# Output sums of an FFT filter and Swish layer: tokens stationary, or output weights stationary and turned by DMA

## The chip, the cores and the metric

The kernel runs on one core of a Trainium2 chip. The metric is the device time of one execution in microseconds. Three runs of the kernel before gave 775.34 to 776.41 us, with a median of 775.49 us. A core has five engines that run side by side, each with its own instruction queue taken in order: TensorE (PE; its weight loads are shown as PEld), VectorE (DVE), ScalarE (ACT), GpSimd (POOL) and SyncE (SP), which here only issues DMAs.

## The reference, cut to what matters

```python
def _attn_ref(x, filt_r, filt_i):            # x: 8 x 3008 x 256
    X = np.fft.rfft(x, axis=1)
    Y = X * (filt_r + 1j * filt_i)[None, :, :]
    return np.fft.irfft(Y, n=x.shape[1], axis=1)

def _moe_ref(x, w_in, w_out, beta):          # x: 24064 x 256, d_ff = 2048
    h = x @ w_in
    g = h / (1.0 + np.exp(-beta * h))
    return g @ w_out                         # 24064 x 256, float32
```

A long convolution along the sequence of each batch (the mixing) is followed by a two-layer network on every token.

## The kernel before, in words

**The network, which sets the pace.** The 24064 tokens are 47 blocks of 512 (`TB`). A block has 16 steps, one for each group of 128 hidden features (`NFB`), so there are 752 steps in all (`NSTEP`), and the main loop runs over them in order. Step `s` of block `i` forms the hidden values of one group: two matmuls of 512 columns into `hps` (line L784; four shorter ones where a block holds tokens of two batches), then ScalarE's activation into `gT` (L793). Two steps later (`lags`) the output sums take this `gT` (L802): four matmuls, one for each 128 tokens, with `gT` as the stationary operand and 256 columns of `wout_sb` streamed, into one of two accumulators of the block, `acc[i, 0]` and `acc[i, 1]`. Each is one bank, and the pool `opsum` has three. After the last group of a block, at step 16k + 1, `out_block` copies both accumulators to `ost` on VectorE (L112) and SP stores them to the output (L761 or L763).

**The mixing, woven in.** The transform of one batch is cut into short products that are planned into the steps of the batch before it. `at(step, fn, ...)` puts a call into the list of a step; the main loop runs a step's list after its hidden matmuls and before its output sums. Let `o` be the first step of the batch before (a multiple of 16); steps of a batch are counted from it. The stages are:

- `load_x` (L171): POOL issues the loads of x.
- `s1` (L564): products on x, evacuated to `a1` (one buffer). `a2_load` (L580): SP issues eight transposing DMAs from `a1` to `a2`, two for each quarter.
- `s2` (L591, L605 to L610): products, then three VectorE operations that apply the filter, then an addition on POOL that makes `yh`.
- `s3` (L623): products on `yh`, evacuated to `z`; after each six rows of the spectrum SP stores `z` to a scratch tensor `d` in DRAM (L630, written d<-z).
- `zz_load` (L635): SP loads `d` back in another order, in four quarters, each when the stores have landed. `s4` (L645): products on `zz`, evacuated to `y`, from which the next hidden values come.

For batches 3 to 7, `s2` stands at steps 4, 8 and 12 of each 16 up to step 60, `s3` six steps later (so the last is at 66), `zz_load` at 70, `s4` at 80 to 92, `a2_load` at 82. Batch 2 differs only in its first six `s2`. Batch 1, in the first 80 steps, has `s2` about two steps apart from step 23 to 46, `s3` five steps after it, `zz_load` at 54 and `s4` from 66. Batch 0 is mixed before the main loop.

**What sets the order.** Each engine takes its instructions in the order in which the code emits them. So SP's queue mixes output stores, d<-z stores, zz loads and transposing DMAs, and POOL's mixes the `yh` additions with the issues of x loads. An instruction that waits holds up all behind it on its queue, though not on other engines. The pool `wst` (three buffers of 4 KB a partition, tag `ws`) serves the loads of the output weights at the start, and nothing later.

The last block (steps 736 to 751) has its own ending in `out_last`.

Of the kernel before, what the change touches and what calls it, by code (L numbers as in the profile page):

```python
# [10 lines left out]
P = 128  # L11
# [4 lines left out]
F32 = mybir.dt.float32  # L16
BF16 = mybir.dt.bfloat16
I32 = mybir.dt.int32

TWO_PI = 2.0 * math.pi  # L20

# [15 lines left out]
def kernel(  # L37
# [10 lines left out]
    nc = tc.nc  # L48

    B, S, D = x.shape  # L50
# [50 lines left out]
    wout_sb = wpool.tile([P, NFB, D], BF16, name="wout_sb", tag="wout_sb")  # L101
# [4 lines left out]
    st = {}  # L106

    def evac(dst, src, on_act, scale=None):
        if on_act:
            nc.scalar.activation(dst, src, ACT.Copy, scale=1.0 if scale is None else scale)  # L110
        elif scale is None:
            nc.vector.tensor_copy(dst, src)  # L112
        else:
            nc.vector.tensor_scalar_mul(dst, src, scale)  # L114
# [23 lines left out]
    def small(name, dt=F32):  # L138
        return sp.tile([P, 1], dt, name=name, tag=name)
# [8 lines left out]

    ip = sp.tile([P, 1], I32, name="ip", tag="ip")
    warm = small("warm")  # L150
# [44 lines left out]
    def shift_and(name, sh, mask, eng=None):  # L195
        t = small(name, I32)
        eng = eng or nc.vector
# [150 lines left out]
    wst = ctx.enter_context(tc.tile_pool(name="wstage", bufs=3, **tw))  # L348
# [337 lines left out]
    for b in range(1, B):  # L686
        o = first_step[b - 1]
        if b == 1:
            at(1, z_late, 1, 0)
            at(2, z_late, 1, 1)  # L690
            s1_steps(1, range(16), [4 + (2 * i + 1) // 3 for i in range(16)], False, (1, 4, 7, 10, 13))
            for i, r in enumerate((3, 4, 5, 6)):
                at(r, f_late, 1, i // 2, i % 2)
            for g in range(NG):
                at(o + 16, a2_load, 1, g)
            for hh, z0, f0 in ((2, (6, 9), (12, 15, 16, 17)), (3, (17, 18), (19, 20, 21, 22))):
                for e in range(NDC):
                    at(z0[e], z_late, hh, e)
                for i, r in enumerate(f0):
                    at(r, f_late, hh, i // 2, i % 2)  # L700
            s23_steps(1, [o + r for r in (23, 25, 27, 29, 31, 34, 36, 38, 40, 42, 44, 46)], 5, 1)
            for h in range(J // JG):
                at(o + 54, zz_load, 1, h)
            s4_steps(1, [o + 66 + (i * 12) // 15 for i in range(16)], 2)
            at(0, scale_wout, 2 * WG)
            at(0, load_wout, 3 * WG)
            at(1, scale_wout, 3 * WG)
            if B > 2:
                for g in range(4):
                    at(o + 24 + 3 * g, load_x, 2, g)  # L710
                late = (54, 55, 56, 57, 58, 59, 60, 61, 66, 67, 68, 70, 72, 73, 74, 76)
                s1_steps(2, range(16), [o + r for r in late], False)
                for g in range(NG):
                    at(o + 80, a2_load, 2, g)
                if B > 3:
                    for g in range(4):
                        at(o + (62, 68, 88, 92)[g], load_x, 3, g)
            continue
        base = [o + 16 * n + s for n in range(4) for s in (4, 8, 12)]
        if b == 2:  # L720
            base[:6] = [o + r for r in (8, 12, 19, 22, 26, 29)]
        s23_steps(b, base, 6, False)
        for h in range(J // JG):
            at(o + 70, zz_load, b, h)
        s4_steps(b, [o + 80 + (i * 13) // 15 for i in range(16)], False)
        if b + 1 < B:
            early = [o + 16 * n + s for n in range(4) for s in (7, 13)]
            late = [o + s for s in (66, 67, 69, 70, 72, 73, 75, 76)]
            s1_steps(b + 1, range(16), early + late, False)
            for g in range(NG):  # L730
                at(o + 82, a2_load, b + 1, g)
            if b + 2 < B:
                for g in range(4):
# [12 lines left out]
    def acc_of(i, tb):  # L746
        h = tb if i == NBLK - 1 and tb == 3 else tb // 2
        if (i, h) not in acc:
            acc[i, h] = opsum.tile([P, 2, D], F32, name="acc", tag="acc")
        return acc[i, h]  # L750

    def out_block(i):
        ost = ostp.tile([P, 4, D], F32, name="ost", tag="ost")
        rows = out[i * TB : (i + 1) * TB, :].rearrange("(c p) d -> p c d", p=P)
# [8 lines left out]
        nc.sync.dma_start(rows, ost[:])  # L763

    def out_last(i, tb, ost):
        rows = out[i * TB : (i + 1) * TB, :].rearrange("(c p) d -> p c d", p=P)
        if tb == 1:
            evac(ost[:, :2, :], acc[i, 0][:], True)
            nc.sync.dma_start(rows[:, :2, :], ost[:, :2, :])
        elif tb > 1:  # L770
            evac(ost[:, tb, :], acc_of(i, tb)[:, tb % 2, :], False)
            (nc.scalar if tb == 2 else nc.sync).dma_start(rows[:, tb, :], ost[:, tb, :])

    for s in range(NSTEP + 4):
        if s < NSTEP:
            i, fb = divmod(s, NFB)
            t0 = i * TB
            hps = hpsum.tile([P, TB], F32, name="hps", tag="hps")
            pos = t0
            while pos < t0 + TB:  # L780
                b, n0 = divmod(pos, S)
                ln = min(S - n0, t0 + TB - pos)
                for dc in range(NDC):
                    nc.tensor.matmul(  # L784
                        hps[:, pos - t0 : pos - t0 + ln],
                        lhsT=win_sb[:, dc, fb * P : (fb + 1) * P],
                        rhs=ys[b][:, dc, n0 : n0 + ln],
                        start=(dc == 0),
                        stop=(dc == NDC - 1),
                    )  # L790
# [9 lines left out]
        for i, fb, tb in outs.get(s, ()):  # L800
            lone = i == last and tb > 1
            nc.tensor.matmul(  # L802
                acc_of(i, tb)[:, tb % 2, :],
                lhsT=blk[i * NFB + fb][:, tb * P : (tb + 1) * P],
                rhs=wout_sb[:, fb, :],
                start=(fb == 0 and (tb % 2 == 0 or lone)),
                stop=(fb == NFB - 1),
                skip_group_check=True,
            )
            if fb == NFB - 1:  # L810
                if i == last:
                    out_last(i, tb, ost)
                elif tb == 3:
                    out_block(i)
# [1 line left out]
_INS = ['x', 'filt_r', 'filt_i', 'moe_w_in', 'moe_w_out', 'moe_beta']  # L816
_OUTS = [((24064, 256), 'float32')]
# [25 lines left out]
```

## Time and profile before

| what | value |
|---|---|
| median of three runs | 775.49 us |
| the profiled execution's own time | 775.0 us |
| its span on the core | 773.0 us |
| granted TensorE clock | 0.999 |
| busy: PE, PEld, DVE, ACT, POOL | 757.8, 549.6, 433.3, 552.3, 151.1 us |
| DMA: moved, mean rate | 77.74 MB, 101 GB/s |
| transposing DMAs of `a2_load` | 56, median 1.287 us to issue, 2.8 us to landing |

The span is the time between the first and the last instruction of the profiled execution, and the execution's own time is some 2 us longer. Times in a timeline count from the start of the span. A line names the source line, the engine, the operation, the tiles written and read, and their shape. SPq and POOLq are DMA issues on the queues of SP and POOL; their duration is that of the issue, not of the transfer. "Landing" is the time from the issue to the end of the transfer. Matmuls are pipelined, so that the durations of two neighbours overlap; the distance between starts is what counts.

### The profile page before, as it was taken

The numbers are of one execution on the slowest core, as the hardware profiler recorded it, in microseconds if no ns is written. First come the engines' busy times: TensorE is split into PE (matmuls) and PEld (weight loads), VectorE is DVE, ScalarE is ACT, GpSimd is POOL, SyncE is SP. The second block draws the span as 40 slices with busy tenths as digits, with TensorE's granted clock in tenths as the row PEclk, the third lists the DMA queues.
The fourth block names the chain that finished last, engine by engine and source line by source line (L and its number), as shares of the span: only waits on it lengthen the run. The fifth ranks groups of instructions, "written<-read, shape, count | busy, mean of one in ns | idle before, by whom it ended". The sixth has DMA issues, their size and how long they took to land.

```text
span 773.0 us, 15801 instructions
## 1 busy us (share of the span) xinstructions
PE 757.8 (98%) x6286; PEld 549.6 (71%) x6383; DVE 433.3 (56%) x716; ACT 552.3 (71%) x813; POOL 151.1 (20%) x154
## 2 busy tenths in 40 slices
PE   8899999999999999999999999999999999999997
PEld 5677777677776777877778777776777766676665
DVE  8879654765556655667456664566745665321001
ACT  7767877776677766776767776677766777777776
POOL 6804301312012210122101322022200222000000
PEclk9999999999999999999999999999999999999999
DMA  9959475234813258141681317621146111500101
GB/s 199 245 111 154 124 171 114 69 113 88 192 51 88 76 122 176 32 116 50 149 152 64 82 48 178 130 68 48 49 130 137 49 49 48 157 29 28 56 28 55
DMA packets 104125, 77.74 MB, mean 101 GB/s; under 512 B 49692, under 2 KB 97052, under 8 KB 104052
## 3 DMA queue, kind: packets, MB, share of 16 engines
q1 hardware_dynamic: 97652, 63.19, 31.6%
q0 software_dynamic: 4192, 13.40, 10.2%
q8 instruction: 50, 0.82, 0.4%
q10 hardware_dynamic: 2208, 0.14, 0.2%
q14 instruction: 23, 0.19, 0.1%
HBM read 43.46 MB, written 35.65 MB: 102 GB/s over the span
## 4 chain that ended last, share of the span: by engine, by line
PE 96%; ACT 1%; DVE 1%; issue 1%; POOL 0%; DVEq 0%; POOLq 0%
PE acc L802 44%; PE hps L784 39%; PE ps L645 3%; PE ps L564 3%; PE ps L591 3%; PE ps L623 3%; PE sps L444 0%; PE tp L393 0%; ACT aT L110 0%; ACT t L110 0%; ACT y L110 0%; PE ps L398 0%; DVE u L226 0%; DVE pq_t L430 0%; PE sps L423 0%
## 5 line engine op out<-in xcount | busy, mean ns | idle before, releaser
L793 ACT ACTIVATE gT<-hps,beta_sb 128x512 bf16<-128x512 f32 x752 | 516.8, 687 | 208.1 <-PE hps L784 184.3
L802 PE MATMUL acc<-wout_sb,gT 128*128 128x256 bf16 x3008 | 453.2, 272 | 2.3
L784 PE MATMUL hps<-y,win_sb 128*128 128x512 bf16 (+7 forms) x1633 | 427.4, 350 | 0.1
L802 PEld LDWEIGHTS <-gT 128*128 128x128 bf16 x3008 | 281.0, 98 | 101.9 <-issue 0.9
L610 POOL TENSOR_TENSOR yh<-a_t,b_t 128x512 bf16<-128x512 f32 x84 | 106.6, 1269 | 421.4 <-DVE b_t L609 421.0
L784 PEld LDWEIGHTS <-win_sb 128*128 128x128 bf16 x1728 | 164.7, 98 | 24.5 <-DVE y L114 0.3
L112 DVE COPY ost<-acc 128x512 f32<-128x512 f32 (+1 forms) x94 | 60.0, 680 | 139.8 <-PE acc L802 139.7
L114 DVE TENSOR_SCALAR y<-ps 128x376 bf16<-128x376 f32 (+2 forms) x128 | 63.3, 510 | 62.2 <-PE ps L645 59.1
L605 DVE TENSOR_TENSOR a_t<-ps,fr_sb 128x512 f32<-128x512 f32 x84 | 58.1, 692 | 67.7 <-PE ps L591 67.2
L112 DVE CAST a<-ps 128x384 bf16<-128x384 f32 x107 | 59.1, 557 | 57.2 <-PE ps L564 46.8
L606 DVE SCALAR_TENSOR_TENSOR b_t<-ps,fi_sb 64x512 f32<-64x512 f32 x84 | 58.2, 693 | 1.1
L609 DVE TENSOR_TENSOR b_t<-ps,fi_sb 64x512 f32<-64x512 f32 x84 | 57.4, 684 | 1.1
L112 DVE CAST z<-ps 128x512 bf16<-128x512 f32 x72 | 49.4, 686 | 1.9 <-PE ps L623 1.0
L645 PEld LDWEIGHTS <-zz 96*128 96x128 bf16 x448 | 29.7, 97 | 22.9
L564 PEld LDWEIGHTS <-xg 94*128 94x128 bf16 x448 | 30.4, 97 | 19.9 <-DMA xg<-in_x_dram 0.2
L564 PE MATMUL ps<-t,xg 94*128 94x96 bf16 x448 | 36.7, 205 | 0.7
L645 PE MATMUL ps<-t,zz 96*128 96x94 bf16 x448 | 34.7, 205 | 1.2
L623 PE MATMUL ps<-yh,t 128*128 128x256 bf16 x168 | 32.1, 273 | 0.4
L591 PE MATMUL ps<-a,t 128*128 128x256 bf16 x168 | 32.1, 273 | 0.4
L623 PEld LDWEIGHTS <-t 128*128 128x128 bf16 x168 | 16.2, 98 | 17.7 <-issue 0.6
L591 PEld LDWEIGHTS <-t 128*128 128x128 bf16 x168 | 16.1, 98 | 16.1
L171 POOL DMA_DIRECT2D xg<-in_x_dram x24 | 12.5, 523 | 54.9 <-PE ps L564 54.9
(95 smaller groups left out, 175.9 us busy)
## 6 DMA issues: line engine op xcount, KB each, us to landing
out_dram<-ost SPq DMA_DIRECT2D x42, 512.0 KB, 3.0
d<-z SPq DMA_DIRECT2D x28, 384.0 KB, 3.7
zz<-d SPq DMA_DIRECT2D x28, 384.0 KB, 6.8
xg<-in_x_dram POOLq DMA_DIRECT2D x24, 384.0 KB, 4.9
out_dram<-ost SPq DMA_DIRECT2D x9, 256.0 KB, 3.4
ws<-in_moe_w_out_dram SPq DMA_DIRECT2D x4, 512.0 KB, 7.8
fr_sb<-in_filt_r_dram SPq DMA_DIRECT2D x12, 128.0 KB, 4.3
fi_sb<-in_filt_i_dram SPq DMA_DIRECT2D x12, 128.0 KB, 4.3
```

The lines of the kernel that those rows point to most:

```text
L112: nc.vector.tensor_copy(dst, src)
L114: nc.vector.tensor_scalar_mul(dst, src, scale)
L564: nc.tensor.matmul(ps[:, m * KP : (m + 1) * KP], lhsT=xg[b, g][:NP, m0 + m, e * P : (e + 1) * P], rhs=t1[:], start=True, stop=True,)
L591: nc.tensor.matmul(ps[:, e, :], lhsT=t2[:, k0 + e, :], rhs=st["a2", b, g][:, kk + e, :], start=True, stop=True,)
L605: nc.vector.tensor_tensor(a_t[:], ps[:], fr_sb[:, ks, :], ALU.mult)
L606: nc.vector.scalar_tensor_tensor(b_t[:M], ps[M:], -1.0, fi_sb[M:, ks, :], ALU.mult, ALU.mult)
L610: nc.gpsimd.tensor_tensor(yh[:], a_t[:], b_t[:], ALU.add)
L623: nc.tensor.matmul(ps[:, e, :], lhsT=t3[:, 2 * i + e, :P], rhs=yh[:, e, :], start=True, stop=True)
L645: nc.tensor.matmul(ps[:, e, :NP], lhsT=zz[:, j0 % JG + e, dc * P : (dc + 1) * P], rhs=t4[:], start=True, stop=True,)
L784: nc.tensor.matmul(hps[:, pos - t0 : pos - t0 + ln], lhsT=win_sb[:, dc, fb * P : (fb + 1) * P], rhs=ys[b][:, dc, n0 : n0 + ln], start=(dc ...
L793: nc.scalar.activation(gT[:], hps[:], ACT.Silu, scale=beta_sb[:, fb : fb + 1])
L802: nc.tensor.matmul(acc_of(i, tb)[:, tb % 2, :], lhsT=blk[i * NFB + fb][:, tb * P : (tb + 1) * P], rhs=wout_sb[:, fb, :], start=(fb == 0 an ...
```

## The change

For all blocks but the last, the output sums swap their operands. The stationary operand is now a 128 x 128 piece of the output weights, and the 512 tokens of `gT` are streamed: two matmuls of 512 columns a step instead of four of 256. The sums then stand turned, with output features on the partitions and tokens along them, and have to be turned back before they are stored:

1. `out_turn(i)`, at step 16k + 1. For each of the two accumulators VectorE copies it to `of`; POOL splits its 32-bit values into two planes of 16-bit halves, `pl`; SP issues a transposing DMA of 128 x 1024 16-bit values from `pl` to `xb`.
2. `out_block(i)`, planned eleven steps later. POOL joins the two planes of `xb` to 32-bit values in `ost`, in two copies, and SP stores `ost` as before.

`of`, `pl` and `xb` take the three buffers of `wst` in turn. The four quarters of `a2_load` are no longer issued together: they stand four steps apart, from step 80 or 82 (17, 19, 24 and 30 for batch 1). The steps of `s1` for batch 1 move by one. The last block keeps the old form.

```diff
-            s1_steps(1, range(16), [4 + (2 * i + 1) // 3 for i in range(16)], False, (1, 4, 7, 10, 13))
+            s1_steps(1, range(16), [5 + (2 * i + 1) // 3 for i in range(16)], False, (1, 4, 7, 10, 13))
...
-                at(o + 16, a2_load, 1, g)
+                at(o + (17, 19, 24, 30)[g], a2_load, 1, g)
...
-                    at(o + 80, a2_load, 2, g)
+                    at(o + 80 + 4 * g, a2_load, 2, g)
...
-                at(o + 82, a2_load, b + 1, g)
+                at(o + 82 + 4 * g, a2_load, b + 1, g)
...
-    lags = {i: (2, 2, 2, 2) for i in range(NBLK)}
+    lags = {i: (2, 2) for i in range(NBLK)}
...
+    def out_turn(i):
+        of = wst.tile([P, NDC, TB], F32, name="ws", tag="ws")
+        pl = wst.tile([P, NDC, 2, TB], U16, name="ws", tag="ws")
+        xb = wst.tile([P, 2, 4, D], U16, name="ws", tag="ws")
+        for dc in range(NDC):
+            evac(of[:, dc, :], acc[i, dc][:].rearrange("p a d -> p (a d)"), False)
+            nc.gpsimd.tensor_copy(
+                pl[:, dc],
+                of[:, dc, :].bitcast(U16).rearrange("p (t q) -> p q t", q=2),
+            )
+            nc.sync.dma_start_transpose(
+                xb[:, :, :, dc * P : (dc + 1) * P].rearrange("p q c d -> p (q c) d"),
+                pl[:, dc].rearrange("p q t -> p (q t)"),
+            )
+        st["xb", i] = xb
+
     def out_block(i):
+        xb = st.pop(("xb", i))
         ost = ostp.tile([P, 4, D], F32, name="ost", tag="ost")
...
         for h in range(2):
-            evac(ost[:, 2 * h : 2 * h + 2, :], acc[i, h][:], False)
+            cs = slice(2 * h, 2 * h + 2)
+            nc.gpsimd.tensor_copy(
+                ost[:, cs, :].rearrange("p c d -> p (c d)").bitcast(U16).rearrange("p (c q) -> p c q", q=2),
+                xb[:, :, cs, :].rearrange("p q c d -> p (c d) q"),
+            )
...
+        for i, fb, q in outs.get(s, ()):
+            gT = blk[i * NFB + fb]
+            if i < last:
+                nc.tensor.matmul(
+                    acc_of(i, q)[:].rearrange("p a d -> p (a d)"),
+                    lhsT=wout_sb[:, fb, q * P : (q + 1) * P],
+                    rhs=gT[:],
+                    start=(fb == 0),
+                    stop=(fb == NFB - 1),
+                )
+                if fb == NFB - 1 and q == 1:
+                    out_turn(i)
+                    at(s + 11, out_block, i)
+                continue
```

More of the change, by code (lines that the diff above doesn't have):

```diff
@@ L18 @@
 I32 = mybir.dt.int32
+U16 = mybir.dt.uint16
 TWO_PI = 2.0 * math.pi
@@ L744, with acc_of @@
             outs.setdefault(min(s + lag, NSTEP + max(1, tb)), []).append((i, fb, tb))
-    def acc_of(i, tb):
-        h = tb if i == NBLK - 1 and tb == 3 else tb // 2
+    def acc_of(i, h):
         if (i, h) not in acc:
@@ L750, in acc_of, with last_acc @@
         return acc[i, h]
+    def last_acc(tb):
+        return acc_of(NBLK - 1, tb if tb == 3 else tb // 2)
+    def out_turn(i):
[13 more added lines that the diff above has]
+        st["xb", i] = xb
     def out_block(i):
+        xb = st.pop(("xb", i))
         ost = ostp.tile([P, 4, D], F32, name="ost", tag="ost")
-        rows = out[i * TB : (i + 1) * TB, :].rearrange("(c p) d -> p c d", p=P)
         for h in range(2):
-            evac(ost[:, 2 * h : 2 * h + 2, :], acc[i, h][:], False)
+            cs = slice(2 * h, 2 * h + 2)
[3 more added lines that the diff above has]
+            )
         if i < HB:
@@ L762, in out_block @@
             return
-        nc.sync.dma_start(rows, ost[:])
+        nc.sync.dma_start(out[i * TB : (i + 1) * TB, :].rearrange("(c p) d -> p c d", p=P), ost[:])
     def out_last(i, tb, ost):
@@ L770, in out_last @@
         elif tb > 1:
-            evac(ost[:, tb, :], acc_of(i, tb)[:, tb % 2, :], False)
+            evac(ost[:, tb, :], last_acc(tb)[:, tb % 2, :], False)
             (nc.scalar if tb == 2 else nc.sync).dma_start(rows[:, tb, :], ost[:, tb, :])
@@ L799 @@
             ost = ostp.tile([P, 4, D], F32, name="ost", tag="ost")
-        for i, fb, tb in outs.get(s, ()):
-            lone = i == last and tb > 1
+        for i, fb, q in outs.get(s, ()):
[12 more added lines that the diff above has]
+                continue
             nc.tensor.matmul(
-                acc_of(i, tb)[:, tb % 2, :],
-                lhsT=blk[i * NFB + fb][:, tb * P : (tb + 1) * P],
+                last_acc(q)[:, q % 2, :],
+                lhsT=gT[:, q * P : (q + 1) * P],
                 rhs=wout_sb[:, fb, :],
-                start=(fb == 0 and (tb % 2 == 0 or lone)),
+                start=(fb == 0 and (q % 2 == 0 or q > 1)),
                 stop=(fb == NFB - 1),
@@ L810 @@
             if fb == NFB - 1:
[L811 to L814, printed above, removed]
+                out_last(i, q, ost)
 _INS = ['x', 'filt_r', 'filt_i', 'moe_w_in', 'moe_w_out', 'moe_beta']
```

## The prediction

> **What bounds the kernel now.** I read the busy table first, then the chain that ended last, then the groups, and last the timeline around the places where work comes from a DMA. From the page:
>
> ```profile
> span 773.0 us, 15801 instructions
> ...
> PE 757.8 (98%) x6286; PEld 549.6 (71%) x6383; DVE 433.3 (56%) x716; ACT 552.3 (71%) x813; POOL 151.1 (20%) x154
> ...
> PE 96%; ACT 1%; DVE 1%; issue 1%; POOL 0%; DVEq 0%; POOLq 0%
> ...
> L802 PE MATMUL acc<-wout_sb,gT 128*128 128x256 bf16 x3008 | 453.2, 272 | 2.3
> ...
> L610 POOL TENSOR_TENSOR yh<-a_t,b_t 128x512 bf16<-128x512 f32 x84 | 106.6, 1269 | 421.4 <-DVE b_t L609 421.0
> ```
>
> and from the groups with shapes kept apart, which also show smaller ones:
>
> ```profile
> L472 POOL COPY fr_sb<-fr_sb 64x1024 f32<-64x1024 f32 x6 | 6.2, 1038 | 1.6 <-DMA fr_sb<-in_filt_r_dram 1.4
> ```
>
> TensorE carries 96% of the chain; everything else hides under it. So a change can gain only by shortening TensorE's own stream, and loses whatever it makes TensorE wait for. The two POOL lines are the only prices there near the new work.
>
> The timeline of a stretch with no mixing work (columns: start, duration, engine, line) gives TensorE's price:
>
> ```profile
> 657.71 0.59 PE L784 MATMUL hps<-y,win_sb 128*128 128x512 bf16 x2
> ...
> 666.39 0.59 PE L784 MATMUL hps<-y,win_sb 128*128 128x512 bf16 x2
> ```
>
> Ten steps lie between, so a bare step is 0.868 us. It streams 2 x 512 + 4 x 256 = 2048 columns.
>
> The third view is the timeline of the queues around the one transfer that TensorE is about to need, the mixing result zz of batch 6:
>
> ```profile
> 559.25 1.27 POOL L610 TENSOR_TENSOR yh<-a_t,b_t 128x512 bf16<-128x512 f32 x1 [2.64 <-DVE b_t L609]
> 561.87 1.29 DVE L112 COPY ost<-acc 128x512 f32<-128x512 f32 x2 [1.60 <-PE acc L802]
> 563.78 0.37 SPq L630 DMA_DIRECT2D d<-z  x1
> 567.57 3.04 SPq L635 DMA_DIRECT2D zz<-d  x4
> 576.09 0.50 PE L645 MATMUL ps<-t,zz 96*128 96x94 bf16 x8
> ```
>
> and the landing of the first zz quarter alone:
>
> ```profile
> DMA to landing us min/median/max: 4.7/4.7/4.7
> ```
>
> It lands at 567.57 + 4.7 = 572.3, and s4 wants it at 576.1: slack 3.8 us. The same subtraction for batches 1 to 4 and 7 gives 3.3, 2.7, 2.6, 2.3 and 3.2. Batch 5 has no landing for its first quarter; its issue is 8.5 us ahead of s4, and with a 7 us landing I take 1.5. This hidden slack decides the case.
>
> **What the Trainium skill says.** "TensorE: Matmul & The Clock Gate", section "Wait — 56ns, not 53.3ns?": a warm matmul costs N/2.4 + about 2.5 ns. The trace agrees: 2048/2.4 = 853.3 ns, and the other 14.7 ns over six matmuls is 2.4 ns each. "GPSIMD Engine Reference", sections 3.1 and 7: a light one-input body runs at 1.03 cycles an element at 1.2 GHz, and a read whose inner step is above 8 bytes costs about one cycle more. The 1038 ns for 1024 elements fits the first; no row shows the second. "DMA: Bandwidth & Descriptors", section "Queues, rings and completion order": one issuer's descriptors are consumed in ring order on each engine, so a store issued behind transposes has their data ahead of it.
>
> **The change part by part, on the profiled span.**
>
> *TensorE.* 736 of 752 steps get two 512-column matmuls for four of 256: the same columns, 1472 fewer matmuls. At 2.4 ns that is **-3.6 us** (2.9 to 5.2 at 2.0 and 3.5 ns). The lost weight loads were already under matmuls: in a bare step PEld is shorter than PE.
>
> *VectorE.* Two copies of 128x512 f32 per block before and after (686 ns each), at the same point: 0. Cover: their accumulator pair is one of three banks, as before.
>
> *Pool.* Per block two splits (1024 16-bit elements, read step 4 bytes) and two joins (1024, inner read step 2048 bytes). Split: 1.04 us by the copy row. Join: 1038 + 1024/1.2 = **1.9 us**, an estimate from the copy row and the GPSIMD page. Bounds: 1.04 if the step is free; 2.6 for the join and 1.75 for the split if the loop is the page's 1.9-cycle one. Load: 46 x (2 x 1.04 + 2 x 1.9) = 270 us on 151, Pool then near half busy, so it isn't short of time; its order is what matters. It is in order, and the built order for batches from 2 on is yh of s2 at step 60, joins of step 60, an x load (0.52, batches 2 to 5), splits of step 65.
>
> *SP.* Two transposes of 128x1024 per block. The row for 128x768 has a median issue of 1.287 us (2.8 to landing), so 1.287 x 8/6 = 1.72 us each, 158 us for 92: SP has room. Its order: transposes of step 65, then the last d<-z of the batch (step 66), then the four zz loads. The transposes wait for the splits, and the d<-z and zz queue behind them.
>
> *The zz chain, batch 6.* yh ends 560.52; two joins to 564.3; first split to 565.4 (its VectorE copy was ready at 562.6); first transpose issued by 567.1, second by 568.8; d<-z issues at 568.8 instead of 563.78: 5.0 late. Transpose data still in the rings: 0.5 (issue to landing leaves a 1.5 us tail, of which d<-z's own start covers most; 0 to 1.5). Sum 5.5; 6.0 with the x load. From d<-z to zz nothing changes.
>
> Loss = lateness - slack. Batch 2: 6.0 - 2.7 = 3.3; 3: 3.4; 4: 3.7; 5: 4.5; 6: 5.5 - 3.8 = 1.7; 7: 2.3. Sum 18.9.
>
> *Batch 1* runs its spectra two steps apart, so Pool has only 0.85 us free between yh's and s3 follows yh by about 0.9. Joins of step 28 put in 3.8: 3.8 - 0.85 - 0.9 = 2.1 lost at s3. Splits of step 33: 2.1 - 0.85 = 1.2. Joins of step 44: 2.1. Its zz chain then adds about 0.4, since TensorE is already late. Sum 5.8.
>
> *Covered elsewhere.* yh of step 52 is ready at 551.48 and joins plus splits of that block end at 544.97 + 3.8 + 2.1 = 550.9: no wait, by 0.6. The spaced a2 loads queue behind the transposes of step 81: first split done at about 579.9, two transposes of 1.72 and eight of 1.29 with gaps (1.34) end near 594, landing by 597; s1 overwrites a1 some 31 us after the zz issue, at 599: no wait, by 2. Without that cover each costs its lateness once a batch.
>
> Sum: 773.0 - 3.6 + 18.9 + 5.8 = 794.1. Runs have a median of 775.49, 2.4 above the span: **796.5**.
>
> **The rivals.**
>
> *The step is free (join 1.04).* d<-z is then 3.3 + 0.5 = 3.8 late, 4.3 with the x load: losses 1.6, 1.7, 2.0, 2.8, 0, 0.6 and 2.2 for batch 1, 10.9 in all: 773.0 - 3.6 + 10.9 + 2.4 = **782.7**. For it: 2-byte reads of a contiguous outer run. Against: the inner step is 2 KB.
>
> *Pool is the bound (2.6 and 1.75).* d<-z is 7.6 or 8.1 late: 31.5 for batches 2 to 7, about 10.6 for batch 1: **814**, and yh of step 52 now ends after its s3 is due (553.7 + 1.27 against 554.6), so more. Against: the copy row is well below 1.75.
>
> *The cover holds.* If the lateness stays under the slack, only TensorE's saving is left: 775.5 - 3.6 = **771.9**. It needs transposes far cheaper than scaled: with free joins, the splits start at 562.6, end the first at 563.6, and the lateness is 2t - 0.2, below 2.3 only where a transpose's issue t is under about 1.2 us. For it: part of the 1.287 may be a fixed cost. Against: eight back to back took 11 to 12 us with the DMA engines nine tenths busy, so data, too, sets that pace.
>
> That the change doesn't do what it says is ruled out by the built order: two matmuls per step, and the queues as told.
>
> **How the numbers follow.** 0.2% (1.6 us) is about what a measurement of this kernel can tell from no change. Chances: strided joins, 788 to 804: 0.50; free step, 779 to 788: 0.22; Pool slower, 804 to 825: 0.14; cover holds, 770 to 774: 0.11; near no change: 0.03. Faster 0.11, same 0.03, slower 0.86. The range takes the first two cases and the lower half of the third: 779 to 814.
>
> **What would show it.** L802's successor at two matmuls of 128x512 a step and a bare step of 0.863. Join rows near 1.9 and splits near 1.04 on Pool. Between the last d<-z and the evacuation of acc a gap grown from 1.9 to about 7 us, and TensorE waits on DMA zz of 2 to 5 us, once a batch; in batch 1 waits of s3 on Pool's yh. It is wrong if transposes issue much faster than 1.7 us, if zz lands quicker once no x load runs beside it, or if TensorE waits on something that the before trace hides, such as acc banks or a2.

## The result, and the profile after

The changed kernel takes 797.53 us (median of four runs, 796.54 to 799.47) against 775.61 for the kernel before beside it. The ratio is 1.028, with a 95% interval of 1.026 to 1.031. The forecast was 796.5, 1 us away. The size of the loss was right, its place was wrong. In the medians further down, two executions (at 1781 and 810 us), each more than 1.5% above the fastest of its kernel, are left out as slow.

From the page of the kernel after:

```profile
span 796.5 us, 13236 instructions
...
PE 764.4 (96%) x4819; PEld 407.6 (51%) x4911; DVE 433.4 (54%) x716; ACT 552.5 (69%) x813; POOL 344.5 (43%) x338
...
PEclk9999999799999999999999999989999999999999
...
L826 PE MATMUL acc<-gT,wout_sb 128*128 128x512 bf16 x1414 | 431.3, 381 | 3.5 <-issue 0.2
...
L776 POOL COPY ost<-ws 128x1024 uint16<-128x1024 uint16 x92 | 103.0, 1150 | 114.8 <-DMA ws<-ws 80.7
L761 POOL COPY ws<-ws 128x1024 uint16<-128x1024 uint16 x92 | 93.2, 1044 | 113.1 <-DVE ws L113 113.1
```

The span has grown by 23.5 us. Pool's busy time rose as forecast in kind, from 151 to 345 us. The split (L761) takes 1.04 us, but the join (L776) only 1.15, not 1.9. PEclk has a 7 and an 8 where it had been full: TensorE was idle long enough there to lose its clock.

What TensorE waits for, longest sums first (columns: us in total, times, longest one):

```profile
PE ps L565 <- DVE a L113: 6.4, 1, 6.4
PE ps L592 <- DVE a L113: 2.6, 1, 2.6
PE ps L646 <- DMA zz<-d: 2.5, 5, 1.3
PE ps L592 <- DMA a<-a: 2.0, 2, 1.9
PE ps L624 <- POOL yh L611: 2.0, 2, 1.3
```

The forecast wanted waits of s4 (L646) on zz of 2 to 5 us once a batch. They are there, but the longest is 1.3 us. The longest wait by far is one that no step of the forecast has: s1 (L565) waits 6.4 us, once, for an evacuation into `a1`.

To see all losses I compared the start of ScalarE's 752 activations of hidden values, one for each step, in the two traces. Their distance from step to step, after minus before, adds up so (us; steps of the main loop, 0 to 751):

| place | forecast | after |
|---|---|---|
| TensorE's own stream | -3.6 | -2.4 |
| batch 1, steps 0 to 80 | 5.8 | 4.4 |
| s1 of batch 3 and what follows, steps 80 to 100 | 0 | 11.4 |
| waits of s4 on zz, batches 2 to 7 | 18.9 | 3.3 |
| s2 of batch 6 and s1 of batch 7, steps 466 to 481 | 0 | 7.0 |
| sum | 21.1 | 23.6 |

Two places that the forecast costed at nothing hold 18.4 us.

**The larger one.** The queues around step 80, timeline of the kernel after, cut to the lines that matter (columns: start, duration, engine, line; in brackets the idle time of the engine and what ended it). L765 are the output transposes, L776 the joins, L784 the output store, L581 the a2 loads, and L172 is an x load:

```profile
110.61 5.00 SPq L765 DMA_TRANSPOSE ws<-ws  x2
111.51 0.51 POOL L172 DMA_DIRECT2D xg<-in_x_dram  x1
120.05 2.25 POOL L776 COPY ost<-ws 128x1024 uint16<-128x1024 uint16 x2 [8.04 <-DMA ws<-ws]
122.33 1.13 SPq L784 DMA_DIRECT2D out_dram<-ost  x2
123.55 3.65 SPq L581 DMA_TRANSPOSE a<-a  x2
128.40 2.61 SPq L765 DMA_TRANSPOSE ws<-ws  x2
131.05 10.48 SPq L581 DMA_TRANSPOSE a<-a  x6
143.26 0.56 DVE L113 CAST a<-ps 128x384 bf16<-128x384 f32 x1 [15.39 <-DMA a<-a]
143.87 0.48 PE L565 MATMUL ps<-t,xg 94*128 94x96 bf16 x4 [6.44 <-DVE a L113]
```

and the same place in the kernel before:

```profile
115.67 12.22 SPq L580 DMA_TRANSPOSE a<-a  x8
...
129.67 0.56 DVE L112 CAST a<-ps 128x384 bf16<-128x384 f32 x1 [6.25 <-DMA a<-a]
```

`a1` has one buffer. s1 of batch 3 begins at step 87 and may not write `a1` before the a2 loads of batch 2 have read it all. VectorE, which does that evacuation, already stood 6.25 us for it before the change, with TensorE still covered. Now it stands 15.39 us and TensorE runs dry. Two delays add up on SP. First, the output store at 122.33 waits for joins, which wait for a pair of transposes that needs about 8 us to land; the first a2 load stands behind that store and goes 7.9 us later than before. Of these, 4.4 are the lateness that TensorE already has by then, with which `a1` is filled; about 3.5 are the store's. Second, the eight a2 loads, once a single run of 12.2 us, now have the block's own transposes in their middle, and the last one's issue ends at 141.5 instead of 127.9. In the plan, the last two quarters of batch 2 even stand at steps 88 and 92, behind the first s1 of batch 3 at 87.

The idle time costs more than itself. Windows of the kernel after (the column after POOL is PEclk, then DMA share and GB/s):

```profile
138.00:140.00 2.00, 0.00 (x0) 0.00 (x0) 0.00 (x0) 0.21 (x1) 0.00 (x0) 1.00 0.80 153
...
144.00:146.00 2.00, 2.00 (x10) 0.95 (x9) 1.94 (x4) 0.00 (x0) 0.00 (x0) 0.50 0.00 0
```

The Trainium skill, "TensorE: Matmul & The Clock Gate", section "What's actually happening", says that after an idle window of about 3.4 us the array falls to half its clock. The trace agrees: idle from 137.4, half clock from about 142 to 152. TensorE was busy for 6.8 us of that stretch, so about 3.4 us of the 11.4 are the clock's (an estimate from these windows).

**The smaller one** is the same wait four batches later, for batches 6 and 7; four x loads leave together at 503.6 to 505.1 just when a2 is to be loaded. The change itself has put them there. Two of the four before (L174 to L176 are x loads of the last batch):

```profile
472.78 0.53 POOL L174 DMA_DIRECT2D xg<-in_x_dram  x1 [5.63 <-PE ps L564]
...
479.19 0.51 POOL L175 DMA_DIRECT2D xg<-in_x_dram  x1
```

and two of the same loads after:

```profile
501.61 2.03 POOL L761 COPY ws<-ws 128x1024 uint16<-128x1024 uint16 x2 [5.54 <-DVE ws L113]
503.58 0.53 POOL L175 DMA_DIRECT2D xg<-in_x_dram  x1
...
505.11 0.51 POOL L176 DMA_DIRECT2D xg<-in_x_dram  x1
```

Before, an x load left as soon as s1's matmuls had freed its buffer, in steps 438 to 445. Now the splits stand ahead of it on Pool and wait for VectorE's copies at the end of a block, so that all four leave in steps 452 to 454. In the same way an x load of batch 3 left at 110.4 before, ahead of the a2 loads of batch 2, and leaves at 129.3 after, in their midst.

**Transposes beside other transfers.** One pair of output transposes close to these four x loads, and one in a stretch without x loads (instructions, then their landing), both of the kernel after:

```profile
L765 SPq DMA_TRANSPOSE ws<-ws x2: 1232/1275/1318, 502.7 to 504.0; - x2
...
DMA to landing us min/median/max: 3.6/8.8/14.1
```

```profile
L765 SPq DMA_TRANSPOSE ws<-ws x2: 1243/1288/1332, 603.6 to 604.9; - x2
...
DMA to landing us min/median/max: 3.2/3.3/3.4
```

The second transpose of the first pair landed after 14.1 us, those of the other pair after 3.2 and 3.4. In the whole trace, all 18 pairs after 520 us, where no x is loaded any more, land within 3.8 us. Of the 28 earlier ones, 15 had an x load issued within 7 us before or 3 us after them, and 13 of these 15 have a landing of 5 us or more; of the other 13 only two do, at 5.0 and 5.2 us.

### The profile page after: what moved, and what is told of

The parts are those of the page before. It is cut to its first block, busy times and chain, and to the rows that moved or that the text cites. A ratio compares the mean times of both kernels' runs of the same rounds, so it can differ in the third digit from the quotient of the medians.

```text
span 796.5 us, 13236 instructions
## 1 busy us (share of the span) xinstructions
PE 764.4 (96%) x4819; PEld 407.6 (51%) x4911; DVE 433.4 (54%) x716; ACT 552.5 (69%) x813; POOL 344.5 (43%) x338
## 5 line engine op out<-in xcount | busy, mean ns | idle before, releaser
L807 PE MATMUL hps<-y,win_sb 128*128 128x512 bf16 (+7 forms) x1696 | 443.5, 353 | 1.1
L826 PE MATMUL acc<-gT,wout_sb 128*128 128x512 bf16 x1414 | 431.3, 381 | 3.5 <-issue 0.2
L826 PEld LDWEIGHTS <-wout_sb 128*128 128x128 bf16 x1472 | 132.1, 98 | 79.8 <-issue 1.2
L776 POOL COPY ost<-ws 128x1024 uint16<-128x1024 uint16 x92 | 103.0, 1150 | 114.8 <-DMA ws<-ws 80.7
L761 POOL COPY ws<-ws 128x1024 uint16<-128x1024 uint16 x92 | 93.2, 1044 | 113.1 <-DVE ws L113 113.1
L113 DVE COPY ws<-acc 128x512 f32<-128x512 f32 x92 | 59.2, 685 | 131.2 <-PE acc L826 128.0
L565 PEld LDWEIGHTS <-xg 94*128 94x128 bf16 x448 | 30.6, 98 | 27.7 <-issue 7.8
L565 PE MATMUL ps<-t,xg 94*128 94x96 bf16 x448 | 37.0, 206 | 7.4 <-DVE a L113 6.4
L646 PEld LDWEIGHTS <-zz 96*128 96x128 bf16 x448 | 29.2, 97 | 26.7 <-DMA zz<-d 4.9
L646 PE MATMUL ps<-t,zz 96*128 96x94 bf16 x448 | 34.7, 205 | 2.7 <-DMA zz<-d 2.5
L624 PEld LDWEIGHTS <-t 128*128 128x128 bf16 x168 | 16.4, 99 | 21.2 <-issue 3.0
```

Of the source, the lines that this page charges most:

```text
L565: nc.tensor.matmul(ps[:, m * KP : (m + 1) * KP], lhsT=xg[b, g][:NP, m0 + m, e * P : (e + 1) * P], rhs=t1[:], start=True, stop=True,)
L646: nc.tensor.matmul(ps[:, e, :NP], lhsT=zz[:, j0 % JG + e, dc * P : (dc + 1) * P], rhs=t4[:], start=True, stop=True,)
L761: nc.gpsimd.tensor_copy(pl[:, dc], of[:, dc, :].bitcast(U16).rearrange("p (t q) -> p q t", q=2),)
L776: nc.gpsimd.tensor_copy(ost[:, cs, :].rearrange("p c d -> p (c d)").bitcast(U16).rearrange("p (c q) -> p c q", q=2), xb[:, :, cs, :].rearr ...
L807: nc.tensor.matmul(hps[:, pos - t0 : pos - t0 + ln], lhsT=win_sb[:, dc, fb * P : (fb + 1) * P], rhs=ys[b][:, dc, n0 : n0 + ln], start=(dc ...
L826: nc.tensor.matmul(acc_of(i, q)[:].rearrange("p a d -> p (a d)"), lhsT=wout_sb[:, fb, q * P : (q + 1) * P], rhs=gT[:], start=(fb == 0), st ...
```

## The experiments

All ratios are to the kernel before on the same chip, from the means of the runs, with their 95% interval. The table gives, for each trace, the same differences to the kernel before by place as above; "zz" is the steps around the first s4 of batches 2 to 7, "rest" all other steps.

| kernel | us | steps 0-80 | 80-100 | zz | 466-481 | rest |
|---|---|---|---|---|---|---|
| after | 797.5 | 4.4 | 11.4 | 3.3 | 7.0 | -2.4 |
| a2 loads together | 790.1 | 2.2 | 5.2 | 4.2 | 6.2 | -2.4 |
| neither Pool copies nor transposes | 772.8 | 0.3 | 0.6 | 0.0 | -0.1 | -3.0 |
| Pool copies alone | 779.0 | 2.8 | 2.5 | 0.0 | 0.0 | -2.4 |
| transposes alone | 788.7 | 7.5 | 7.4 | 3.2 | -0.1 | -3.0 |
| x loads later | 790.0 | 4.7 | 8.3 | 4.2 | 0.0 | -2.4 |
| a2 loads earlier | 799.3 | 5.5 | 9.0 | 3.8 | 0.1 | 6.8 |
| transposes two steps later | 788.9 | 4.2 | 11.5 | 0.0 | 0.0 | -2.4 |
| x loads spread | 786.3 | 5.9 | 8.4 | 0.2 | 0.0 | -2.4 |
| a2 loads from another tile | 785.1 | 6.0 | 0.0 | 5.7 | 2.4 | -2.4 |

The time is the median of the runs, the places are from the one trace, so the two agree only to 1 or 2 us.

**The parts of the change.** First, only the new matmuls, with the copies of the accumulators stored as they stand:

```diff
-        pl = wst.tile([P, NDC, 2, TB], U16, name="ws", tag="ws")
-        xb = wst.tile([P, 2, 4, D], U16, name="ws", tag="ws")
...
-        st["xb", i] = xb
+        st["xb", i] = of
```

> The changed kernel without the turn: splits, transposes and joins are left out and the accumulators' copies are stored as they stand, so that the output is not turned back. The stationary weights, the spread a2 loads and the stores eleven steps later stay. All theories that put the loss into the turn: the gain of TensorE alone, 3.6 us less what the accumulator banks take back, so 772 to 776. If the spread of the a2 loads costs by itself: 778 to 790.

Measured: 772.81 us, ratio 0.996 (0.9945 to 0.9975). The new form of the matmuls gains about 3 us, as the forecast's first step said, and everything else that is lost comes with the turning.

Then splits and joins without the transposes:

```diff
-            nc.sync.dma_start_transpose(
-                xb[:, :, :, dc * P : (dc + 1) * P].rearrange("p q c d -> p (q c) d"),
-                pl[:, dc].rearrange("p q t -> p (q t)"),
-            )
-        st["xb", i] = xb
+        st["xb", i] = pl
...
-                xb[:, :, cs, :].rearrange("p q c d -> p (c d) q"),
+                xb[:, h].rearrange("p q t -> p t q"),
```

> The changed kernel with splits and joins but without the transposing DMAs of the output: the joins read the split planes directly, so that the output is not turned back. The prediction's theory (what Pool holds up): half of the loss or more stays, 784 or above. Theory A and B (the transposes on SP's queue and in the DMA engines): 774 to 779, with 1 to 3 us of it from s3 waiting for yh in batch 1.

Measured: 778.99 us, 1.0046 (1.0030 to 1.0063). Pool's copies cost 6.2 us over the kernel without them. Their trace shows s3 waiting three times for Pool's `yh`, 3.5 us in all. Two of these waits, 1.2 us together, are in batch 1, the first of them behind joins as in the forecast. The third, 2.3 us at step 95, is in batch 2 and comes by way of `a1` again: no copy stands ahead of that `yh`, but VectorE's evacuation into `a1` starts only at 135.2, just after the last a2 load has landed (issued at 129.6, 5.5 us). The x load held back by the splits left at 127.8, beside these loads.

And the transposes without Pool's copies:

```diff
-        of = wst.tile([P, NDC, TB], F32, name="ws", tag="ws")
-        pl = wst.tile([P, NDC, 2, TB], U16, name="ws", tag="ws")
+        of = wst.tile([P, NDC, TB], BF16, name="ws", tag="ws")
...
-                pl[:, dc].rearrange("p q t -> p (q t)"),
+                of[:].rearrange("p e t -> p (e t)").bitcast(U16),
...
+        ost = xb[:].rearrange("p q c d -> p (q c d)").bitcast(F32).rearrange("p (c d) -> p c d", d=D)
```

> The changed kernel with the transposing DMAs of the output but without Pool's splits and joins: VectorE writes the accumulators as 16-bit values, both transposes read these 1024 values, and SP stores what they leave, so that the output is not the sums. Theory A and B: most of the loss stays, 788 to 798. The prediction's theory: the joins' and splits' part of the lateness goes, 776 to 783.

Measured: 788.68 us, 1.015 (1.010 to 1.020), so 15.9 us over the kernel with neither. Transposes cost more than twice what Pool's copies do, and the two together (24.7) are about the sum (22.1). By place they don't add up: the 7.0 us at steps 466 to 481 appear in neither. With the copies alone the four x loads leave together there, as in the full change, and meet no output transposes; with the transposes alone they leave in steps 438 to 445, as before. It takes the splits that hold them back and the transposes that they then meet.

The loss of 7.5 us in steps 0 to 80 is larger than in the full change. There a pair of output transposes takes 12.0 us to issue (at 73.5, with x loads at 71.4 and 73.5), and the d<-z store issued at 71.9 lands after 13.8 us (5.8 before). ScalarE's next evacuation into `z` waits for that landing, s3 waits 2.8 us for ScalarE, and TensorE's clock is at half for 6.8 us from 85.5 on.

**The spread of the a2 loads.** They are put together again:

```diff
-                at(o + (17, 19, 24, 30)[g], a2_load, 1, g)
+                at(o + 16, a2_load, 1, g)
...
-                    at(o + 80 + 4 * g, a2_load, 2, g)
+                    at(o + 80, a2_load, 2, g)
...
-                at(o + 82 + 4 * g, a2_load, b + 1, g)
+                at(o + 82, a2_load, b + 1, g)
```

> The changed kernel with one part undone: the four quarters of a2_load are issued together again (step 16 for batch 1, 80 and 82 later), as before the change. Theory A (the trace after: the loss sits where s1 may not overwrite a1 until the last transposing load from it has landed, and the spread puts that load later and behind the block's own transposes): the 11.3 us lost at steps 93 to 96 shrink to 3 or less, the 2.8 us at step 41 go, 797.5 falls to about 784. Theory B (the 24 MB of new transposes slow every DMA, wherever the a2 loads stand): 794 to 799. The prediction's theory (zz late behind joins, splits and transposes): no change, 797.

Measured: 790.12 us, 1.018 (1.016 to 1.021), 7.4 us less. The loss in steps 80 to 100 falls from 11.4 to 5.2 and batch 1's from 4.4 to 2.2; zz waits become a little longer. The last a2 load of batch 2 is now issued by 133.9 instead of 141.5. So the spreading costs 7 us, half of the 13 us that the expectation gave it. What remains at step 80 and at 466 has another cause, though at step 80 the wait is the same: VectorE still stands 10.0 us until the last a2 load has landed.

**The x loads.** The last two x loads of a batch leave 16 to 18 steps later, after the a2 loads:

```diff
-                        at(o + (62, 68, 88, 92)[g], load_x, 3, g)
+                        at(o + (62, 68, 104, 110)[g], load_x, 3, g)
...
-                    at(o + (30, 62, 88, 92)[g], load_x, b + 2, g)
+                    at(o + (30, 62, 104, 110)[g], load_x, b + 2, g)
```

> The changed kernel with only the last two x loads of a batch moved from steps 88 and 92 to 104 and 110, so that they no longer start beside the transposes of step 81 and the a2 loads. Theory C (the transposing loads are late because x loads run beside them): the 6.9 us lost at steps 468 to 479 shrink to 2 or less and the loss at steps 93 to 96 by 3 or more, total 784 to 790. Theory A (place and order on SP's queue alone): 795 to 799.

Measured: 789.96 us, 1.018 (1.017 to 1.020). The loss of 7.0 us in steps 466 to 481 is gone, and 3 us of the one at 80. Waits on zz stay.

Then all of them away from the transposes as far as the plan lets them:

```diff
-                        at(o + (62, 68, 88, 92)[g], load_x, 3, g)
+                        at(o + (60, 104, 120, 136)[g], load_x, 3, g)
...
-                    at(o + (30, 62, 88, 92)[g], load_x, b + 2, g)
+                    at(o + (40, 104, 120, 136)[g], load_x, b + 2, g)
```

> The changed kernel with only the x loads from batch 3 on moved, to steps that lie eight after the output turn of a block (40, 104, 120 and 136; 60 for the first of batch 3), so that none starts within some 4 us of an output transpose. Theory C (a transpose beside an x load takes two to four times as long, 5 to 14 us to land instead of 3.3, and what queues behind it on SP is late): the losses at steps 93 to 96 fall from 11 to 4 or less, that at 468 to 479 from 6.9 to 1 or less, zz waits halve; total 779 to 785. Theory A (order on SP's queue alone): 790 or above.

Measured: 786.27 us, 1.013 (1.011 to 1.015), a little above the expected span of times. Waits on zz are nearly gone too (0.2 us), though SP's order around zz was not touched and Pool lost only the issue of one x load (0.5 us) there. In batch 4 the transposes ahead of d<-z are issued in 2.8 us instead of 5.2, and d<-z leaves 6.1 us after `yh` instead of 9.0. In this trace four pairs of transposes have a landing of 5 us or more, against 15 in the changed kernel. So the x loads made the transposes slow, and slow transposes made both zz and a2 late. The 8.4 us at step 80 stay: there the pair issued at 111.9 still took 6.0 to 6.6 us to land with no x load within 8 us of it, while other transfers (zz loads, output stores) had run just before. I can't say which of them matters.

**The queue behind the transposes.** The output transposes are issued two steps later, behind the last d<-z of a batch:

```diff
+        st["xb", i] = xb
+        st["pl", i] = pl
+
+    def out_send(i):
+        pl, xb = st.pop(("pl", i)), st["xb", i]
+        for dc in range(NDC):
...
+                    at(s + 2, out_send, i)
```

> The changed kernel with only the output transposes issued two steps later, so that the last d<-z store of a batch stands ahead of them on SP's queue. The prediction's theory, at the size that the trace after shows: waits on zz (2.5 us on matmuls and 4.9 on weight loads, partly the same time) go, 3 to 5 us gained, total 792 to 795. If the wait is set elsewhere (joins, DMA load): 797 or above.

Measured: 788.94 us, 1.017 (1.016 to 1.019). I had expected 792 to 795: the zz waits alone, if they are the 3 us of the trace. They are gone, as expected. In addition the loss at 466 to 481 is gone, which was not expected. In this trace the first two a2 loads leave at 496.5, ahead of the output transposes (500.1) and of the four x loads behind these, so that four a2 loads and not six stand behind them; the joins run at 510.8 instead of 518.2 and the last a2 loads leave at 513.6 instead of 522.8, with TensorE about 3 us earlier. The loss at step 80 is untouched. This also prices the zz chain as it stands in the changed kernel: 3 us, not 18.9.

**An earlier start of the a2 loads.**

```diff
-                    at(o + 80 + 4 * g, a2_load, 2, g)
+                    at(o + 78, a2_load, 2, g)
...
-                at(o + 82 + 4 * g, a2_load, b + 1, g)
+                at(o + 78, a2_load, b + 1, g)
```

> The changed kernel with only the a2 loads from batch 2 on moved to step 78, all four quarters together, so that they stand ahead of the output transposes of step 81 on SP's queue and ahead of the x loads. Theory A: the losses at steps 93 to 96 and 468 to 479 fall to 1 to 3 us each, total 781 to 785. Theory B (DMA volume as such): 792 or above. What then stays above 773 is batch 1, Pool's copies and zz.

Measured: 799.33 us, 1.028 (1.025 to 1.031). The expectation failed: I had 781 to 785. The queues of this kernel show why:

```profile
111.90 3.16 SPq L765 DMA_TRANSPOSE ws<-ws  x2
112.80 0.51 POOL L172 DMA_DIRECT2D xg<-in_x_dram  x1
123.84 2.25 POOL L776 COPY ost<-ws 128x1024 uint16<-128x1024 uint16 x2 [10.54 <-DMA ws<-ws]
126.11 1.13 SPq L784 DMA_DIRECT2D out_dram<-ost  x2
127.34 13.17 SPq L581 DMA_TRANSPOSE a<-a  x8
```

The loads stand ahead of the block's transposes now, but behind the output store of the block before. That store waits for the joins, and the joins for a pair of transposes that land only after 10.4 and 10.9 us, with an x load issued 0.9 us after them. A place in the plan says nothing while something that waits stands ahead of it on SP. The loss at 466 is gone, but new ones of 5.1 and 4.0 us appear at steps 186 and 282.

**The wait itself.** The last test leaves every transpose where it is and takes away what s1 waits for: the a2 loads of batches 2 to 7 read a piece of the output weights instead of `a1`.

```diff
-                st["a1", b][:, e, 4 * KG * h : 4 * KG * (h + 1), :].rearrange("p k j -> p (k j)"),
+                (st["a1", b][:, e, 4 * KG * h : 4 * KG * (h + 1), :].rearrange("p k j -> p (k j)")
+                 if b < 2 else
+                 wout_sb[:, 2 * h + e : 2 * h + e + 3, :].rearrange("p f d -> p (f d)")),
```

> The changed kernel, in which the a2 loads of batches 2 to 7 turn pieces of the output weights instead of a1: the same transposes, at the same places in SP's queue and of the same size, but s1 of the next batch has nothing to wait for (the mixing of those batches is then computed from other numbers). My theory, that the changed kernel loses 11.3 us at steps 93 to 96 and 6.9 us at steps 468 to 479 because s1 must not overwrite the single a1 until the last a2 load has read it: both losses go, nothing takes their place, 797.5 - 18.2 = 779.3 us (777 to 783). What stays is batch 1's 4 us and the zz waits of some 3 us; with a TensorE that is earlier the zz waits may grow by 1 or 2. The rival, that the late a2 itself is what is missing: s2 or s3 of the next batch then waits for its landing instead, and the time stays at 790 to 798 us. The forecast of the record, that zz alone costs 18.9 us: no change, 797 us, and the waits on zz grow to what s1's waits had covered.

Measured: 785.09 us, 1.0116 (1.0095 to 1.0137). The loss in steps 80 to 100 is wholly gone:

```profile
130.04 2.61 SPq L767 DMA_TRANSPOSE ws<-ws  x2
132.70 12.09 SPq L581 DMA_TRANSPOSE a<-wout_sb  x6
...
133.46 0.56 DVE L113 CAST a<-ps 128x384 bf16<-128x384 f32 x1 [3.95 <-PE ps L565]
```

SP is as late as ever, the last load ends at 144.8, and VectorE doesn't wait for it (its 3.95 us are for TensorE). So the 11.4 us are the wait for the one buffer of `a1`, clock loss included. At 466 to 481, 4.5 of 7.0 us go; the other 2.4 us are s2, which waits for the late a2 itself, as the rival said. And the waits on zz grow from 3.3 to 5.7 us, and batch 1 by 1.7 us in this trace, where the clock was at half from 86.0 to 89.4: 785 instead of 779.

**A version with all of it.** a2 loads at 78 (16 and 20 for batch 1), x loads later, transposes later, joins at step 16k + 7 (later for the first two blocks), the second accumulator a step behind the first so that each is copied and split when it is complete:

```diff
-    lags = {i: (2, 2) for i in range(NBLK)}
+    lags = {i: (2, 3) for i in range(NBLK)}
...
+                if fb == NFB - 1:
+                    out_turn(i, q)
+                    if q == 1:
+                        at(s + 1, out_send, i)
+                        at({0: 22, 1: 47}.get(i, s + 5), out_block, i)
```

> All of it together: stationary output weights and the full turn, with a2 loads at step 78 (16 and 20 for batch 1), x loads at 104 and 110, output transposes behind the last d<-z, joins at step 16k + 7 in a gap between two yh, and the second accumulator one step behind the first, so that its bank is copied out a step earlier. If the loss is made of these placements: 770 to 777, at or below the kernel before. If DMA volume or Pool's share of work costs as such: 783 or above.

Measured: 780.98 us, 1.007 (1.006 to 1.008), with x loads at 104 and 110: between the two expected spans. Its largest waits are those of s3 for `yh`, 7.6 us in three: joins stand ahead of `yh` on Pool while their transposes are not there. With the spread x loads of above:

```diff
-                        at(o + (62, 68, 104, 110)[g], load_x, 3, g)
+                        at(o + (60, 104, 120, 136)[g], load_x, 3, g)
...
-                    at(o + (30, 62, 104, 110)[g], load_x, b + 2, g)
+                    at(o + (40, 104, 120, 136)[g], load_x, b + 2, g)
```

> The combined version with its x loads at the same quiet steps instead of 62, 104 and 110. Theory C: the two losses left in it (7.6 us at steps 93 to 95 and 4.2 at 126 to 127) shrink to 3 together, total 770 to 774, below the kernel before. If Pool's copies or DMA volume set them: 779 or above.

Measured: 776.78 us, 1.0005 (0.9992 to 1.0018): no difference from the kernel before, and above the 770 to 774 that I had expected. Of the rest, 5.3 us are in steps 80 to 100, where s3 waits 3.6 us for a `yh` behind joins.

**The kernel before, with the second accumulator a step behind:**

```diff
-    lags = {i: (2, 2, 2, 2) for i in range(NBLK)}
+    lags = {i: (2, 2, 3, 3) for i in range(NBLK)}
...
-        for h in range(2):
-            evac(ost[:, 2 * h : 2 * h + 2, :], acc[i, h][:], False)
+        evac(ost[:, 2 * h : 2 * h + 2, :], acc[i, h][:], False)
```

> The kernel before with only its second accumulator one step behind the first, each copied out when it is complete. If the 0.07 us longer step once a block is a wait for the bank of the first accumulator: 46 x 0.074 = 3.4 us gained, 772 to 773. If it is something else: 775.5.

Measured: 774.35 us, 0.9976 (0.9968 to 0.9985). It beats both kernels, the one before by 1.6 us. In the blocks without mixing, the step in which a block's sums begin falls from 0.942 to 0.868 us, the length of its neighbours: it no longer waits for a free accumulator bank. The gain is half of the 3.4 us expected, since only about 20 of the 46 blocks get shorter in the trace.

## Why the prediction was right in size and wrong in place

That the sum met the time to 1 us is luck. It had 15.6 us too much for zz, and nothing for two places that cost 18.4.

**TensorE, -3.6: right for the stream, short by a wait.** A bare step went from 0.868 to 0.863 us, as worked out, and the kernel without turning gains 3.0 us in the column "rest". In the full change 2.4 are left. In blocks without mixing, one step a block, in which the block's sums begin and need both its banks, goes from 0.942 to 1.010 us, which takes the saving back. In the kernel with transposes and no Pool copies this step stays at 0.942, with Pool copies and no transposes it is 0.995 or more. So it was the step "0. Cover: their accumulator pair is one of three banks", for VectorE, that was not quite right: the cover was not complete before either, and Pool's copies uncover more. Why a copy on Pool lengthens the wait was not tried further.

**"Join: 1038 + 1024/1.2 = 1.9 us": failed.** It measured 1.150 us. The cycle more that the Trainium skill, "GPSIMD Engine Reference", section 7, states for a read step above 8 bytes doesn't show here: with an inner step of 2048 bytes the join takes 10% more than the split with 4. The measurement decides.

**"1.287 x 8/6 = 1.72 us each": failed.** The row of the changed kernel has a median of 1.288 us for 128x1024, as the 1.287 for 128x768. Issue time does not scale with size between these two. The working had named this possibility under the rival "the cover holds" and then set it aside.

**The zz chain: the order right, "From d<-z to zz nothing changes" wrong.** In batch 4 of the kernel before (the last line is the landing of the first zz quarter):

```profile
370.48 1.27 POOL L610 TENSOR_TENSOR yh<-a_t,b_t 128x512 bf16<-128x512 f32 x1 [2.65 <-DVE b_t L609]
375.01 1.30 SPq L630 DMA_DIRECT2D d<-z  x1
378.39 0.51 POOL L171 DMA_DIRECT2D xg<-in_x_dram  x1 [6.17 <-PE ps L564]
379.02 2.02 SPq L635 DMA_DIRECT2D zz<-d  x4
...
DMA to landing us min/median/max: 6.0/6.0/6.0
```

and after:

```profile
386.19 1.27 POOL L611 TENSOR_TENSOR yh<-a_t,b_t 128x512 bf16<-128x512 f32 x1 [2.62 <-DVE b_t L610]
387.41 2.24 POOL L776 COPY ost<-ws 128x1024 uint16<-128x1024 uint16 x2
390.11 2.03 POOL L761 COPY ws<-ws 128x1024 uint16<-128x1024 uint16 x2
...
391.19 5.23 SPq L765 DMA_TRANSPOSE ws<-ws  x2
396.51 0.53 SPq L631 DMA_DIRECT2D d<-z  x1
399.67 1.74 SPq L636 DMA_DIRECT2D zz<-d  x4
...
DMA to landing us min/median/max: 3.6/3.6/3.6
```

The order is the forecast one: yh, joins, splits, transposes, d<-z. d<-z leaves 9.0 us after yh's end against 3.3 before, so 5.8 late, close to the 5.5 forecast for this batch; but there two errors cancel, since the joins took 2.2 us and not 3.8, and the two transposes, beside an x load, 5.2 and not 3.4. What makes the loss small comes after: from d<-z's issue to the landing of the first zz quarter it is 10.0 us before and 6.8 after. That gives back 3.2 us, the slack of 2.3 covers most of the rest, and the batch loses 0.4.

Batches 2 and 3 are alike: d<-z 5.9 late in both, 0.4 and 0.6 lost. Batch 5 loses 1.5, the largest, as in the forecast. In batches 6 and 7, with no x load near, d<-z is 2.8 and 2.9 late; they lose nothing and 0.5. Why the transfers are quicker was not tested. In the kernel before, an x load leaves 0.5 to 0.6 us ahead of zz in batches 2 to 4, and in the kernel after none does. The working named this as a sign that it would be wrong. But batch 6, without x loads in both kernels, gains 1.6 us too, so this can't be all of it.

So 3.3 us stand where the sum had 18.9. The rival "the step is free" had 10.9 with batch 1; it too kept the transposes at 1.72 and the transfers behind them as before.

**Batch 1, 5.8: 4.4, half by another wait.** s3 does wait for `yh` behind the joins of step 28 (0.9 us at step 34). The 2.8 us at steps 41 and 42 begin with s2's wait for its last a2 quarter, which the change moved from step 16 to 30; its first load left at 73.2, beside x loads, and took 8.6 us to land. With the quarters together the wait is gone.

**"Covered elsewhere ... s1 overwrites a1 some 31 us after the zz issue, at 599: no wait, by 2": this is the step that failed.** It took the plan of the later batches, in which a2 stands 12 steps after zz and s1 21 after that. For batch 2, a2 stands at step 80 and s1 at 87; the last two quarters were spread to behind it. It also took eight transposes at the pace of one run and put nothing ahead of them but the block's own pair, though the output store, which now waits for joins and so for transposes, stands ahead as well. And it assumed that x loads only cost Pool their 0.52 us, and left their own times as they were. The result is 18.4 us. The working did say that it would be wrong if TensorE waited for a2; the trace of before shows the place, in VectorE's wait of 6.25 us for `a<-a` ahead of 129.67.

**The causes, in order of what the runs show.** s1's wait for the one buffer of `a1`, shown by taking it away: 11.4 and some 4.5 us. What made it late: the spreading of a2 (7.4 us), transposes slowed by x loads (11 us with the zz waits they explain), and stores that wait on SP; these overlap and don't add up. Pool's copies cost some 6 us alone, in part ahead of `yh` and in part through x loads that they hold back. Left open: why zz lands quicker than before, how an x load slows a transpose, what slows the pair at step 80 without one, and the rest of 5 us in the best version of the change.

## What to carry to other kernels

Before an operation is costed at nothing because its buffer comes free in time, look at every place where that buffer is reused, the shortest distance first, and at who already waits there: an idle engine in front of a DMA, harmless today, is the slack that the change spends. On an in-order queue a store that begins to wait for a new chain delays everything planned behind it, so moving the later instruction ahead in the plan does not help while that store still stands in front of it. And an engine that is far from busy still sets when the transfers that it issues start: here the splits on Pool moved x loads onto the a2 loads. A sum that meets the measured time is no proof of its terms; compare the two traces step by step.

## What I had not expected of the hardware

A transposing DMA of 128x1024 16-bit values lands in 3.1 to 3.8 us where no x loads run, and in up to 14.1 us with x loads near it; issuing a pair took 2.6 to 2.8 us in the first case and up to 6.2 in the second. Moving x loads away brought the pairs with a landing of 5 us or more from 15 down to 4. An idle TensorE lost half its clock about 4.5 us after its last work and had it back at 152, 8 us after its return, with a gap of 1.3 us in between. The Pool copy of 1024 16-bit values with an inner read step of 2048 bytes costs 1.150 us, hardly more than the one with 4 bytes.
